# Cross attention and a gated feed-forward on one core: the transposed scores of batches 0 and 1 in one four-bank visit

## The chip, the cores and the metric

The kernel runs on one core of a Trainium2 chip. The metric is the device time of one execution in microseconds (us); the time of a kernel is the median of its runs. A profile is one further execution, recorded by the hardware profiler; its span goes from the first to the last instruction.

The engines are named as the profile names them: PE (matrix products; PEld its weight loads), DVE (vector), ACT (scalar functions), POOL (general), SP (here only an issuer of DMAs). Each works through its own instructions in order and waits on semaphores of the others.

## The reference

For each of B = 8 batches and H = 8 heads, `x` is 512 x 64 and `state` is 32 x 64:

```python
scale = 1.0 / np.sqrt(D)
a  = softmax(scale * x @ state.T)        # 512 x 32
xread = a @ state                        # 512 x 64
a2 = softmax(scale * state @ x.T)        # 32 x 512, the transposed scores
sread = a2 @ x                           # 32 x 64
h = concat([xread, sread])               # 544 rows per batch, heads side by side: 512 columns
out = (sigmoid(h @ w_gate) * (h @ w_val)) @ w_out    # d_ff = 1536
```

The output has 8 x 544 = 4352 rows of 512 floats.

## The kernel before

**Tiling.** The program is written out by hand: the order of the calls in the source is the order on each engine. One *step* belongs to each batch b = 2..7, and one more, b = 8, to the 256 rows of `sread` of all batches. A step is a loop over f = 0..11 (L696 to L744), one *group* for each 128 columns of d_ff. In a group PE makes `gv_mm(b, f)` (L275): gate and value for 128 columns by 512 rows, four 128x512 matmuls, and `out_mm(b - 1, f)` (L305), four matmuls of the output product of the batch before. In the last two steps `out_mm` comes first in each group. ACT makes the tanh of the gate (`gv_th`, L290), DVE multiplies it with the value (`gv_glu`, L295), and after every third group ACT moves an output bank to `res` (L318), from which SP writes 256 KB to DRAM (L320).

**The transposed scores** of a batch k ride in those groups. They go through these functions:

- `cT_mm(k)` (L175): eight matmuls with a 64x32 tile of PE's array each, four by two tiles, into two PSUM banks (e = 0, 1).
- `cT_max(k, e)` (L185): DVE takes the maximum of a bank (`cm`, L188) and makes the bias `nb` (L190).
- `cT_exp(k, e)` (L192): ACT writes the exponentials to `cE` and their sums to `cs` (L196).
- `cT_nrm(k, e)` (L198): DVE takes the reciprocal `rc` of the sums (L201), and POOL multiplies it in and writes `cN` (L204).
- `c_dma(k)` (L206): two DMA transposes on SP's queue, `cN` to `Eb` (L209).
- `sr_mm(k)` (L211): sixteen matmuls of 64 columns, `Eb` with `x`; `sr_cp` (L219) copies the two halves of the result to `XS`, one on ACT and one on DVE (L221). `XS` of all batches is what step 8 works on.

The tiles `cE`, `cs`, `nb`, `cN` and `Eb` come from a pool with two buffers of each name, so a third one waits until an earlier one has been read.

**Where they stand.** Batch b + 1 is done in the last five groups of step b (`col`, L385). Batches 0 and 1 are left for step 7: `col(0, t)` in groups 0 to 4, `col(1, t)` in groups 3 to 7, so that in groups 3 and 4 both are at work. Their order within a group is batch 0 first:

```python
for k in range(2):
    if 0 <= f - 3 * k < 5:
        col(k, f - 3 * k)
    elif f == 8 + 3 * k:
        sr_mm(k, SWP)
        sr_cp(k, 0, act)
        sr_cp(k, 1, vec)
```

`sr_mm(7)` stands in group 9 of step 7, its copies in group 10.

**PSUM.** Eight banks: two for gate and value (GV: one group's worth), one for the output (OU), four that rotate (SWP), one more (AT). In step 7 the scores of batches 0 and 1 and the `sr` results take SWP banks. `out_mm` starts a new output bank in groups 0, 3, 6 and 9, and has only the one bank OU, so it waits until ACT's `res` copy has emptied it.

Of the kernel before, what the change touches and what calls it, by code (L numbers as in the profile page):

```python
# [16 lines left out]
def kernel(  # L17
# [14 lines left out]
    nc = tc.nc  # L32
    B, H, S, D = x.shape
# [30 lines left out]
    AT, OU, GV, SWP = (p_at, "at"), (p_out, "outp"), (p_gv, "gv"), (p_sw, "swp")  # L64
    xfs, xbs, xTs = {}, {}, {}
    Es, E1s, Ebs, abs_, aTs, SWs, glus = {}, {}, {}, {}, {}, {}, {}
    vec, act, pool = nc.vector.tensor_copy, nc.scalar.copy, nc.gpsimd.tensor_copy
# [42 lines left out]
    def at_xT_dma(b):  # L110
        xT = xT_tile(b)
        for c in range(4):
            nc.sync.dma_start_transpose(xT[:, :, c], xbs[b][:, c].rearrange("p h d -> p (h d)"))

    def S_mm(b, i, place, jjs=(0, 1)):
        if jjs[0] == 0:
            held["S", b, i] = place[0].tile((128, 4, 2, 2, Ns), FP, name="Sp", tag=place[1])
        ps = held["S", b, i]
        for jj in jjs:
            for c in range(4):  # L120
                nc.tensor.matmul(ps[:, c, :, jj], xTs[b][:, 2 * i + jj, c], sTz[:, b, 2 * i + jj], start=True, stop=True)  # L121

    def S_max(b, i):

        if b not in E1s:
            E1s[b] = ap_.tile((128, 4, 2, 4, Ns), FP, name="E1")
        ps = held["S", b, i].rearrange("p c e j n -> p (c e) j n")
        mx = held["mx", b, i] = ap_.tile((128, 8, 2), FP, name="mx")
        nc.vector.tensor_reduce(mx, ps, AX.X, ALU.max)  # L129

    def S_sub(b, i):

        mx, ps = held["mx", b, i], held["S", b, i].rearrange("p c e j n -> p (c e) j n")
        nc.vector.tensor_tensor(halfE(b, i), ps, mx.unsqueeze(3).to_broadcast((128, 8, 2, Ns)), ALU.subtract)  # L134

    def S_exp(b, i):
        nc.scalar.activation(halfE(b, i), halfE(b, i), AF.Exp, scale=scale)  # L137
# [4 lines left out]
    def n_sum(b, i):  # L142
        rs = ap_.tile((128, 8, 2), FP, name="rs")
        nc.vector.tensor_reduce(rs, halfE(b, i), AX.X, ALU.add)  # L144
        ri = held["ri", b, i] = ap_.tile((128, 8, 2), FP, name="ri")
        nc.vector.reciprocal(ri, rs)  # L146

    def n_mul(b, i, eng, lo=0, n=4):
        if b not in abs_:
            abs_[b] = ap_.tile((128, 4, 2, 128), BF, name="ab")  # L150
        ri, ce = held["ri", b, i], slice(2 * lo, 2 * lo + 2 * n)
        eng.tensor_tensor(abs_[b].rearrange("p c e (j n) -> p (c e) j n", n=Ns)[:, ce, 2 * i:2 * i + 2],  # L152
                          halfE(b, i)[:, ce], ri[:, ce].unsqueeze(3).to_broadcast((128, 2 * n, 2, Ns)), ALU.mult)
# [17 lines left out]
    def aT_dma(b):  # L171
        for c in range(4):
            nc.sync.dma_start_transpose(aT_tile(b)[:, c], abs_[b][:, c].rearrange("p e k -> p (e k)"))

    def cT_mm(b, places):  # L175

        pss = [p[0].tile((128, 512), FP, name="cTp", tag=p[1]) for p in places]
        for j in range(4):
            for e in range(2):
                rows = slice(e * 64, (e + 1) * 64)  # L180
                nc.tensor.matmul(pss[e][j * Ns:(j + 1) * Ns], sTz[rows, b, j, e],  # L181
                                 xTs[b][rows, j].rearrange("p c t -> p (c t)"), start=True, stop=True)
        held["cT", b] = pss

    def cT_max(b, e):  # L185

        mx = ap_.tile((128, 1), FP, name="cm")
        nc.vector.tensor_reduce(mx, held["cT", b][e], AX.X, ALU.max)  # L188
        nb = held["nb", b, e] = ap_.tile((128, 1), FP, name="nb")
        nc.vector.tensor_scalar(nb, mx, -scale, None, op0=ALU.mult)  # L190

    def cT_exp(b, e):  # L192

        ex = held["cE", b, e] = ap_.tile((128, 512), FP, name="cE")
        cs = held["cs", b, e] = ap_.tile((128, 1), FP, name="cs")
        nc.scalar.activation(ex, held["cT", b][e], AF.Exp, bias=held["nb", b, e], scale=scale, accum_out=cs)  # L196

    def cT_nrm(b, e, eng):  # L198

        rc = ap_.tile((128, 1), FP, name="rc")  # L200
        nc.vector.reciprocal(rc, held["cs", b, e])  # L201
        if ("cN", b) not in held:
            held["cN", b] = ap_.tile((128, 2, 512), BF, name="cN")
        eng.tensor_scalar(held["cN", b][:, e], held["cE", b, e], rc, None, op0=ALU.mult)  # L204

    def c_dma(b):  # L206
        Ebs[b] = ap_.tile((128, 4, 2, 128), BF, name="Eb")
        for e in range(2):
            nc.sync.dma_start_transpose(Ebs[b][:, :, e], held["cN", b][:, e])  # L209

    def sr_mm(b, place):  # L211
        sr = held["sr", b] = place[0].tile((128, 4, 2, Ns), FP, name="srp", tag=place[1])
        Eb = Ebs[b].rearrange("p c e (j n) -> p c e j n", n=Ns)
        for j in range(4):
            for c in range(4):
                nc.tensor.matmul(sr[:, j], xbs[b][:, c, 2 * j:2 * j + 2].rearrange("p h d -> p (h d)"),  # L216
                                 Eb[:, c, :, j], start=(c == 0), stop=(c == 3))

    def sr_cp(b, e, cp):  # L219
        rows = slice(e * 64, (e + 1) * 64)  # L220
        cp(XS[rows, :, b * Ns:(b + 1) * Ns], held["sr", b][rows, :, e])  # L221
# [46 lines left out]
    def sw_cp(b, lo, w, e, cp):  # L268
        cp(*sw_left.pop((b, lo, w, e)))  # L269
# [115 lines left out]
    def col(b, t):  # L385

        if t == 0:
            cT_mm(b, (AT, SWP) if b > 1 else (SWP, SWP))
            cT_max(b, 0)
        elif t == 1:  # L390
            cT_max(b, 1)
            cT_exp(b, 0)
        elif t == 2:
            cT_exp(b, 1)
        elif t == 3:
            cT_nrm(b, 0, nc.gpsimd)
        else:
            cT_nrm(b, 1, nc.gpsimd)
            c_dma(b)

    def row(b, t):

        if t == 0:
            S_mm(b, 0, AT)
            S_max(b, 0)
        elif t == 1:
            S_sub(b, 0)
            S_mm(b, 1, SWP)
            S_max(b, 1)
        elif t == 2:  # L410
            S_sub(b, 1)
            S_exp(b, 0)
        elif t == 3:
            S_exp(b, 1)
            n_sum(b, 0)
            n_mul(b, 0, nc.gpsimd)
        elif t == 4:
            n_sum(b, 1)
            n_mul(b, 1, nc.gpsimd)
        else:  # L420
            aT_dma(b)
# [274 lines left out]
    for b in range(2, B + 1):  # L696
        nb = b + 1 if b + 1 < B else None
        for f in range(NF):

            v, q = divmod(f, 6)  # L700
            if nb is not None and q == 0:
                sw_wide(nb, v)
                sw_cp(nb, v, 0, 0, act)
                sw_cp(nb, v, 0, 1, act)
            ahead = nb is not None and q == 0
            for first in (ahead, not ahead):
                if first:
                    gv_mm(b, f, SWP if b == B and f % 2 else GV)
                    gv_th(b, f)
                    gv_glu(b, f)  # L710
                elif b < B or f < 9:
                    out_mm(b - 1, f)
            if nb is not None:
                if q == 0:
                    sw_cp(nb, v, 1, 0, vec)
                if q in (1, 3, 4):
                    k = max(q + 1, 3)
                    sw_cp(nb, v, k // 2, k % 2, act)
                if f == 10:
                    sr_cp(b, 0, act)  # L720
                    sr_cp(b, 1, vec)
                if 0 <= f - (b < 4) < 6:
                    row(nb, f - (b < 4))
                elif f >= 7:
                    col(nb, f - 7)
                if f == (6 if b > 3 else 3) and nb + 2 < B:
                    load_x(nb + 2, nc.sync, 4 if nb + 3 == B else 1)
                if f == (1 if b > 2 else 6) and nb + 1 < B:
                    cast_x(nb + 1, pool, 0, 4)
                    cast_x(nb + 1, pool, 4, 4)  # L730
                    at_xT_dma(nb + 1)
            if b < B and f == 9:
                sr_mm(b, SWP)
            if b == B - 1:
                if f == 10:
                    sr_cp(b, 0, act)
                    sr_cp(b, 1, vec)
                for k in range(2):
                    if 0 <= f - 3 * k < 5:
                        col(k, f - 3 * k)  # L740
                    elif f == 8 + 3 * k:
                        sr_mm(k, SWP)
                        sr_cp(k, 0, act)
                        sr_cp(k, 1, vec)  # L744
    for k in range(6):
        out_mm(B, k)
    out_last(B - 1, 3)
# [30 lines left out]
```

## Time and profile before

| | us |
|---|---|
| median of 3 runs | 232.07 |
| lowest and highest run | 231.16, 232.13 |
| the profiled execution's own time | 230.65 |
| its span, first to last instruction | 228.9 |

| engine | busy in the span, us |
|---|---|
| PE | 219.1 |
| ACT | 143.1 |
| DVE | 138.0 |
| POOL | 71.4 |

Step 7 fills about 176 to 199.5 us of the span, step 8 the time from there to 218 us. In a row of the timeline stand the start, the time that the group of instructions takes, the engine, the line, the operation and its tiles, the count, and in brackets how long the engine sat idle just before and what ended that. A matmul's time includes the way through the array: four 128x512 matmuls show 1.03 us, but the next ones start 0.86 us after them. A row that counts x3 where four were issued has lost a record. In a row of the chain stand the start, the time, and the engine with its tile and line.

### The profile page before, as it was taken

To read this page: it belongs to the slowest core of one execution; us is meant where nothing else is said; L and a number is where in the kernel's file an instruction comes from. 1 tells how busy PE (TensorE), PEld (TensorE's weight loads), DVE (VectorE), ACT (ScalarE), POOL (GpSimd) and SP (SyncE) were. 2 spreads that over 40 slices of the span, in tenths; PEclk is the share of its full clock that TensorE was granted. 3 is DMA by queue.
4 is the path that set the end of the run, shared out by engine and by line. 5 is a ranking of instruction groups with operands and counts; after the bars stand their busy time and mean duration, and the time that the engine had idled before them with its cause. 6 is when DMAs were issued, how large, how long until landed. Compare 5 with 4: busy or idle time off the path is not lost.

```text
span 228.9 us, 5007 instructions
## 1 busy us (share of the span) xinstructions
PE 219.1 (96%) x1885; PEld 111.5 (49%) x1911; DVE 138.0 (60%) x266; ACT 143.1 (63%) x288; POOL 71.4 (31%) x77
## 2 busy tenths in 40 slices
PE   8868999999999999999999999999999999999994
PEld 7653444434444444444444444445444434566744
DVE  0889779766587557666766577648755664422311
ACT  3588787677575866676767767584857655422411
POOL 3986371240507080307130533031301355000001
PEclk9999999999999999999999999999999999999999
DMA  6999979935794374842443766313121312411114
GB/s 215 269 201 285 206 88 182 269 85 126 209 292 134 61 181 94 246 148 74 92 126 83 238 84 142 89 46 87 57 46 75 99 37 69 116 39 77 46 26 115
DMA packets 47271, 29.49 MB, mean 129 GB/s; under 512 B 29872, under 2 KB 42544, under 8 KB 47248
## 3 DMA queue, kind: packets, MB, share of 16 engines
q1 hardware_dynamic: 40096, 21.84, 36.5%
q0 software_dynamic: 6864, 7.14, 17.0%
q8 instruction: 15, 0.25, 0.4%
q10 hardware_dynamic: 288, 0.20, 0.3%
q14 instruction: 8, 0.07, 0.1%
HBM read 18.35 MB, written 8.91 MB: 119 GB/s over the span
## 4 chain that ended last, share of the span: by engine, by line
PE 84%; DMA 7%; ACT 2%; issue 2%; POOL 2%; SPq 1%; DVE 0%; ACTq 0%
PE outp L314 36%; PE gvp L283 34%; PE swp L231 5%; PE gvp L286 5%; DMA wg<-in_moe_w_gate_dram 4%; DMA xf<-in_x_dram 2%; PE srp L216 2%; PE Sp L121 1%; SPq L74 1%; PE outp L334 1%; PE cTp L181 1%; POOL cN L204 1%; ACT res L318 1%; POOL xb L91 1%; ACT SW L269 1%
## 5 line engine op out<-in xcount | busy, mean ns | idle before, releaser
L298 DVE SCALAR_TENSOR_TENSOR glu<-th,gvp 128x512 bf16<-128x512 f32 (+1 forms) x108 | 70.3, 656 | 69.1 <-ACT th L293 52.8
L314 PE MATMUL outp<-wo,glu 128*128 128x512 bf16 x370 | 95.5, 379 | 1.7 <-issue 0.3
L283 PE MATMUL gvp<-aT,SW 128*128 128x512 bf16 x384 | 96.6, 379 | 0.3 <-DVE aT L169 0.3
L293 ACT ACTIVATE th<-gvp 128x512 f32<-128x512 f32 (+1 forms) x108 | 61.8, 576 | 51.2 <-PE gvp L283 41.4
L283 PEld LDWEIGHTS <-SW 128*128 128x128 bf16 x384 | 36.3, 98 | 44.8 <-issue 3.1
L314 PEld LDWEIGHTS <-glu 128*128 128x128 bf16 x396 | 36.5, 98 | 40.8 <-issue 3.2
L204 POOL TENSOR_SCALAR cN<-cE,rc 128x512 bf16<-128x512 f32 x16 | 24.9, 1564 | 66.2 <-DVE rc L201 53.4
L269 ACT CAST SW<-swp 128x512 bf16<-128x512 f32 x74 | 41.0, 586 | 3.5 <-PE swp L231 2.5
L152 POOL TENSOR_TENSOR ab<-E,ri 128x512 bf16<-128x512 f32 x16 | 16.7, 1047 | 48.4 <-DVE ri L146 21.7
L318 ACT ACTIVATE res<-outp 128x512 f32<-128x512 f32 x33 | 19.7, 597 | 16.8 <-PE outp L314 16.6
L269 DVE CAST SW<-swp 128x512 bf16<-128x512 f32 x22 | 14.7, 681 | 1.0 <-PE swp L231 1.0
L91 POOL CAST xb<-xf 128x1024 bf16<-128x1024 f32 (+1 forms) x14 | 13.6, 986 | 4.9 <-DMA xf<-in_x_dram 4.9
L196 ACT ACTIVATE cE<-cTp,nb 128x512 f32<-128x512 f32 x16 | 11.1, 694 | 0.8 <-POOL cN L204 0.8
L144 DVE TENSOR_REDUCE rs<-E 128x16 f32<-128x512 f32 x16 | 10.8, 675 | 0.7 <-ACT E L137 0.7
L188 DVE TENSOR_REDUCE cm<-cTp 128x1 f32<-128x512 f32 x16 | 10.9, 682 | 0.4 <-PE cTp L181 0.4
L137 ACT ACTIVATE E<-E 128x512 f32<-128x512 f32 x16 | 10.1, 637 | 1.6 <-DVE E L134 1.6
L129 DVE TENSOR_REDUCE mx<-Sp 128x16 f32<-128x512 f32 x16 | 10.7, 674 | 0.4 <-PE Sp L121 0.4
L134 DVE TENSOR_TENSOR E<-Sp,mx 128x512 f32<-128x512 f32 x16 | 10.9, 684 | 0.1
L325 POOL DMA_DIRECT2D out_dram<-res x2 | 1.1, 550 | 30.1 <-ACT res L318 30.1
L231 PE MATMUL swp<-wg,sTc 64*32 64x512 bf16 (+1 forms) x192 | 8.4, 328 | 0.2
L348 PE MATMUL warm<-ones 128*128 128x128 bf16 x87 | 7.6, 256 | 1.0 <-DVE ones L429 1.0
L231 PEld LDWEIGHTS <-sTc 64*32 64x32 bf16 x384 | 4.8, 91 | 7.4 <-issue 4.7
(62 smaller groups left out, 134.2 us busy)
## 6 DMA issues: line engine op xcount, KB each, us to landing
out_dram<-res SPq DMA_DIRECT2D x31, 256.0 KB, 2.4
xf<-in_x_dram SPq DMA_DIRECT2D x12, 256.0 KB, 4.8
xf<-in_x_dram SPq DMA_DIRECT2D x3, 1024.0 KB, 6.3
wo<-in_moe_w_out_dram POOLq DMA_DIRECT2D x3, 512.0 KB, 8.9
wv<-in_moe_w_val_dram POOLq DMA_DIRECT2D x2, 512.0 KB, 9.1
wg<-in_moe_w_gate_dram POOLq DMA_DIRECT2D x2, 512.0 KB, 10.1
xf<-in_x_dram POOLq DMA_DIRECT2D x2, 512.0 KB, 8.0
xf<-in_x_dram POOLq DMA_DIRECT2D x1, 1024.0 KB, 12.8
```

The costliest lines, as they stand in the source:

```text
L91: cp(xbs[b].rearrange("p c h d -> p h c d")[:, lo:lo + n], xfs[b][:, lo:lo + n])
L152: eng.tensor_tensor(abs_[b].rearrange("p c e (j n) -> p (c e) j n", n=Ns)[:, ce, 2 * i:2 * i + 2], halfE(b, i)[:, ce], ri[:, ce].unsqueeze ...
L196: nc.scalar.activation(ex, held["cT", b][e], AF.Exp, bias=held["nb", b, e], scale=scale, accum_out=cs)
L204: eng.tensor_scalar(held["cN", b][:, e], held["cE", b, e], rc, None, op0=ALU.mult)
L231: nc.tensor.matmul(pss[e][j * Ns:(j + 1) * Ns, o:o + n], sTc[rows, b, j] if b > 1 else sTz[rows, b, j, e], (wg, wv)[w][rows, j, lo:lo + n] ...
L269: cp(*sw_left.pop((b, lo, w, e)))
L283: nc.tensor.matmul(ps, SWs[b][:, g, w, fs], aTs[b][:, :, g], start=(g == 0), stop=(g == 1))
L286: nc.tensor.matmul(ps, (wg, wv)[w][:, j, fs], XS[:, j], start=(j == 0), stop=(j == 3))
L293: nc.scalar.activation(th, held["gv", b, f][0], AF.Tanh, scale=0.5)
L298: nc.vector.scalar_tensor_tensor(glus[b][:, f], held["th", b, f], 1.0, held["gv", b, f][1], ALU.add, ALU.mult)
L314: nc.tensor.matmul(ops[b, c], glus[b][:, f, c * 128:(c + 1) * 128], wo[:, f], start=(f == 0), stop=(f == NF - 1))
L318: nc.scalar.activation(res, ops[b, c], AF.Copy, scale=0.5)
```

## The change

Step 7 no longer uses `col` for batches 0 and 1, but a function of its own, `first01(f)`:

- In group 0 both batches' `cT_mm` are made one after the other, into all four SWP banks. Group 3 has no `cT_mm` any more.
- The maxima go to groups 0 to 3, one in each; the exponentials to groups 1, 3, 4 and 6 (before: 1, 2, 4, 5); the normalisations stay in groups 3, 4, 6 and 7. In group 3 the maximum of batch 1, e = 1 stands ahead of the reciprocal of batch 0, e = 0.
- `sr_mm(7)` and its copies go from groups 9 and 10 to group 5; `sr_mm(0)` goes from group 8 to group 9; `sr_mm(1)` stays in group 11. All three write the bank AT in place of an SWP bank.
- `c_dma(0)` goes from group 4 to group 6; `c_dma(1)` stays in group 7.

```diff
+    def sr_all(b, place):
+        sr_mm(b, place)
+        sr_cp(b, 0, act)
+        sr_cp(b, 1, vec)
+
+    def first01(f):
+
+        if f == 0:
+            for k in range(2):
+                cT_mm(k, (SWP, SWP))
+            cT_max(0, 0)
+        elif f == 1:
+            cT_max(0, 1)
+            cT_exp(0, 0)
+        elif f == 2:
+            cT_max(1, 0)
+        elif f == 3:
+            cT_max(1, 1)
+            cT_exp(0, 1)
+            cT_nrm(0, 0, nc.gpsimd)
+        elif f == 4:
+            cT_exp(1, 0)
+            cT_nrm(0, 1, nc.gpsimd)
+        elif f == 5:
+            sr_all(B - 1, AT)
+        elif f == 6:
+            c_dma(0)
+            cT_exp(1, 1)
+            cT_nrm(1, 0, nc.gpsimd)
+        elif f == 7:
+            cT_nrm(1, 1, nc.gpsimd)
+            c_dma(1)
+        elif f in (9, 11):
+            sr_all(f // 2 - 4, AT)
...
-            if b < B and f == 9:
+            if nb is not None and f == 9:
                 sr_mm(b, SWP)
             if b == B - 1:
-                if f == 10:
-                    sr_cp(b, 0, act)
-                    sr_cp(b, 1, vec)
-                for k in range(2):
-                    if 0 <= f - 3 * k < 5:
-                        col(k, f - 3 * k)
-                    elif f == 8 + 3 * k:
-                        sr_mm(k, SWP)
-                        sr_cp(k, 0, act)
-                        sr_cp(k, 1, vec)
+                first01(f)
```

## The prediction

> **What bounds the kernel now.** First the page: who is busy, and whose work makes up the chain that ended last.
>
> ```profile
> span 228.9 us, 5007 instructions
> PE 219.1 (96%) x1885; PEld 111.5 (49%) x1911; DVE 138.0 (60%) x266; ACT 143.1 (63%) x288; POOL 71.4 (31%) x77
> ...
> PE 84%; DMA 7%; ACT 2%; issue 2%; POOL 2%; SPq 1%; DVE 0%; ACTq 0%
> ```
>
> PE is the bound. Whatever the change does shows only as PE slots saved or added, and as PE idling. So the second view is the stage table, row of step 7 (start and end, length, then busy time of PE, PEld, DVE, ACT and POOL, the granted clock, the DMA share):
>
> ```profile
> 177.90:199.60 21.70, 21.26 (x152) 10.22 (x154) 11.50 (x26) 11.97 (x26) 7.72 (x5) 1.00 0.28 73
> ```
>
> DVE, ACT and POOL are half idle there; PE lacks 0.44 us of being always busy. Third, PE's timeline of that stage:
>
> ```profile
> 177.02 1.03 PE L283 MATMUL gvp<-aT,SW 128*128 128x512 bf16 x4
> 177.98 0.41 PE L181 MATMUL cTp<-xT,sTz 64*32 64x512 bf16 x8
> 178.32 1.04 PE L314 MATMUL outp<-wo,glu 128*128 128x512 bf16 x4
> 179.19 1.03 PE L283 MATMUL gvp<-aT,SW 128*128 128x512 bf16 x4
> ...
> 182.64 1.03 PE L283 MATMUL gvp<-aT,SW 128*128 128x512 bf16 x4
> 183.60 0.41 PE L181 MATMUL cTp<-xT,sTz 64*32 64x512 bf16 x8
> 184.17 0.81 PE L314 MATMUL outp<-wo,glu 128*128 128x512 bf16 x3 [0.16 <-issue]
> 184.82 1.03 PE L283 MATMUL gvp<-aT,SW 128*128 128x512 bf16 x4
> 185.68 1.03 PE L314 MATMUL outp<-wo,glu 128*128 128x512 bf16 x4
> 186.54 1.03 PE L283 MATMUL gvp<-aT,SW 128*128 128x512 bf16 x4
> 187.80 1.02 PE L314 MATMUL outp<-wo,glu 128*128 128x512 bf16 x4 [0.23 <-ACT res L318]
> ```
>
> Four 128x512 matmuls take a slot of 0.86 us (185.68 to 186.54). Two things stand out. A visit to the transposed scores costs 177.98 - 177.02 - 0.86 + 0.34 = 0.44 us of slots, and there are two. And group 6's output product, which could start at 186.54 + 0.86 = 187.40, starts at 187.80: a hole of 0.40 us. The chain of waits says what made the hole:
>
> ```profile
> 183.34 0.61 ACT th L293
> 183.94 0.94 issue
> 184.88 1.57 POOL cN L204
> ...
> 186.48 0.02 ACT cE L196
> 186.50 0.56 issue
> 187.07 0.19 ACT cE L196
> 187.26 0.50 ACT res L318
> ...
> 187.80 1.02 PE outp L314 x4
> ```
>
> Read it backwards. PE needs the output bank that ACT's `res` copy empties; ACT does that copy after the exponential of batch 1, e = 0; that exponential needs a `cE` buffer, and the older of the two is free only when POOL has normalised batch 0, e = 0; POOL waits for the reciprocal on DVE. The 0.94 us that the chain calls issue are DVE's:
>
> ```profile
> 183.97 0.69 DVE L298 SCALAR_TENSOR_TENSOR glu<-th,gvp 128x512 bf16<-128x512 f32 x1 [1.04 <-ACT th L293]
> 184.57 0.15 DVE L201 RECIPROCAL rc<-cs 128x1 f32<-128x1 f32 x1
> 184.64 0.67 DVE L188 TENSOR_REDUCE cm<-cTp 128x1 f32<-128x512 f32 x1
> 185.35 0.15 DVE L190 TENSOR_SCALAR nb<-cm 128x1 f32<-128x1 f32 x1
> ```
>
> So the hole hangs on **where the reciprocal stands in DVE's order of group 3**. Before, it comes directly behind `glu` of group 3, ahead of the maximum.
>
> **The change, part by part.**
>
> *One visit in place of two.* The kernel has such a double set already, early on: sixteen 64x512 matmuls in one go, two sets of weights on the same tiles, and a set of eight close by.
>
> ```profile
> 22.21 0.67 PE L231 MATMUL swp<-wg,sTz 64*32 64x512 bf16 x16 [0.56 <-DMA wg<-in_moe_w_gate_dram]
> 22.81 0.32 PE L369 MATMUL stp<-ident,sb 128*64 128x64 bf16 x8
> ...
> 24.54 0.41 PE L231 MATMUL swp<-wv,sTz 64*32 64x512 bf16 x8
> ```
>
> 0.67 against 0.41 us: the second set costs 0.26. Bounds: one matmul's streaming, 0.86 / 4 = 0.22 us, and a whole second visit, 0.44. I take 0.25. Group 1 thus starts 0.25 us later than before, and all that PE paces up to group 3 with it: `gv_mm` of group 3, its tanh, its `glu`. The second visit's 0.44 us in group 3 goes, but see below: it stands ahead of the hole.
>
> Against this stands a rule of the Trainium skill, TensorE: Matmul & The Clock Gate, section "Part 3: Packing small matmuls", "The mechanism": weight loads overlap running matmuls only where their row group differs. The second set uses the same two row groups as the first, so by that rule it would start like a new visit, 0.44 in place of 0.25, and the sum below would be 0.19 higher. The 0.67 us row speaks against it.
>
> *The order on DVE in group 3.* Now `cT_max(1, 1)` comes ahead of the reciprocal of batch 0, e = 0. So between `glu` of group 3 and that reciprocal stand a reduction and a bias. By the rows above the reduction occupies 184.64 to 185.35 = 0.71 us, and the bias, by the step from one short instruction to the next (184.57 to 184.64), 0.07; if the reciprocal has to wait for its whole length, 0.15. Together 0.78 to 0.86, taken as 0.82. The bias also waits for a free buffer, that is for the exponential of batch 0, e = 1, which ACT now makes in group 3, directly behind the tanh that `glu` waits for too; in the chain 0.78 us pass from one exponential to the copy behind it (186.48 to 187.26), less than `glu` and the reduction take together (183.97 to 185.35), so it is done first. No cost.
>
> Everything behind is a chain of fixed lengths, with no engine that could make it up: POOL 1.57, exponential, `res`, PE. So **PE resumes at 187.80 + 0.25 + 0.82 = 188.87 in place of 187.80, 1.07 us later.** `gv_mm`s of groups 4 and 5 aren't touched: they need only the tanh and `glu` of the group before.
>
> *`sr_mm(7)` goes from group 9 to group 5.* Its cost in a slot, before:
>
> ```profile
> 195.17 0.63 PE L216 MATMUL srp<-Eb,xb 128*128 128x64 bf16 x16
> 195.63 1.03 PE L314 MATMUL outp<-wo,glu 128*128 128x512 bf16 x4
> ```
>
> 0.46 us. Now it stands just ahead of group 6's output product, which is the hole: PE gets there at 187.40 + 0.25 - 0.44 = 187.21, is done with it at 187.67, and idles to 188.87. So the hole shows 1.2 us of idle time, and 0.46 us of work that had to be done anyway now lies in its shadow. It is the one real gain: **-0.46.** Its operand is there: `c_dma(7)` is the last thing of step 6.
>
> *The transposes on SP.* SP's queue holds, in order: the `res` write of group 5, both of batch 0, both of batch 1, the `res` write of group 8. The rows: the end of step 7 and the start of step 8 on PE; batch 1's products and transposes; the time to landing of all sixteen transposes.
>
> ```profile
> 199.55 1.03 PE L314 MATMUL outp<-wo,glu 128*128 128x512 bf16 x3
> 200.61 0.60 PE L286 MATMUL gvp<-XS,wg 128*128 128x256 bf16 x4
> ...
> 190.90 1.57 POOL L204 TENSOR_SCALAR cN<-cE,rc 128x512 bf16<-128x512 f32 x1 [2.27 <-DVE rc L201]
> 192.63 1.56 POOL L204 TENSOR_SCALAR cN<-cE,rc 128x512 bf16<-128x512 f32 x1 [0.17 <-DVE rc L201]
> ...
> 193.69 2.50 SPq L209 DMA_TRANSPOSE Eb<-cN  x2
> ...
> DMA to landing us min/median/max: 2.4/2.4/5.4
> ```
>
> Batch 0: POOL's second product ends at 184.88 + 1.07 + 2 x 1.57 = 189.09, the `res` copy that SP writes first at 187.76 + 1.07 = 188.83; with an estimated 0.6 for that write and 1.25 for the first transpose (half of 2.50) SP gets to the second at about 190.7, and it lands 2.4 later, 193.1. `sr_mm(0)` comes at 188.87 + 8 x 0.86 = 195.8: 2.7 us of slack. Batch 1: POOL's last product, 1.07 later than before, ends at 195.26, its transpose lands at 197.7. `sr_mm(1)`, at 199.55 - 0.46 = 199.09 before, comes 0.6 later: 2 us of slack. Before, the first of this pair (193.69) waited until `sr_mm(0)` had read its `Eb` buffer; now it takes batch 7's, free since group 5. That wait goes and is worth nothing, as POOL is later than it. The write of group 8's `res` is held up as before; `res` has four buffers. No cost.
>
> *The rest.* The exponential of batch 1, e = 1 moves to group 6, where POOL is done (189.09) before the tanh ahead of it is (about 190.9); its wait for POOL goes, but no hole of PE hung on it. The copies to `XS` change groups on engines that are half idle. Bank AT is empty each time: its copies are four groups or two ahead of the next use. The start of step 8 waits for the last `XS` copy as before (200.61 against 199.55 + 0.86 = 200.41: 0.2 us), since group 11 keeps its order.
>
> **The sum:** +0.25 + 0.82 - 0.46 = **+0.61 us**; by the bounds, +0.54 to +0.84. On the profiled execution's 230.65 that gives 231.26; on the median of the runs, 232.07, **232.7**. The profiled execution lies 0.51 under the lowest run, so runs scatter by as much as the change is worth. A difference under 0.5% (1.16 us) can't be told from no change here.
>
> **Rivals.**
>
> *The hole closes.* If POOL's product doesn't decide, the hole (0.40) goes and one visit is saved (0.44 - 0.25 = 0.19): -0.59, so 231.5. For it: fewer PE visits, and the exponentials are spread over more groups. Against it: the exponential of batch 1, e = 0 still stands in group 4, still third in two `cE` buffers, and what frees its buffer comes later on DVE. Chance 0.13.
>
> *The visit saves nothing* (the second set waits for its own weights, as in the rule above): +0.80, 232.9. Against it the x16 row. Chance 0.12.
>
> *Slower by more: the last transpose lands late.* Place: `sr_mm(1)` in group 11 of step 7, and behind it the first `gv_mm` of step 8. It decides from a landing of more than 2.4 + 2.0 = 4.4 us. At the longest in the trace, 5.4, PE waits 1.0 us: +1.6, 233.7. For it: the pair is issued later in time than before. Against it, the transposes in a window early on, where loads of `x` are in flight, and those of step 7, where none is:
>
> ```profile
> DMA to landing us min/median/max: 4.5/4.9/5.4
> ...
> DMA to landing us min/median/max: 2.4/2.4/2.4
> ```
>
> The long landings belong to the early window. Chance 0.09.
>
> *The forecast*, the POOL chain: 0.66.
>
> **How the numbers follow.** Predicted 232.7. The range reaches down to the first rival less half the distance of median and lowest run (231.5 - 0.45 = 231.05), and up to the last, 233.7. Faster by over 0.5% needs the first rival and scatter on top: 0.06. Slower by over 0.5%: the last rival, 0.09, and the upper end of the forecast and of the second with scatter, 0.07: 0.16. Within: 0.78.
>
> **What would show it.** In PE's timeline: x16 `cTp` in about 0.67 us at 178.0, then none; `srp` x16 at about 187.2; behind it `outp` with an idle of about 1 us put down to ACT `res`. On DVE in group 3: `glu`, `cm`, `nb`, `rc`. On ACT: the `cE` of group 4 behind an idle of more than 1 us put down to POOL. On SP: four `Eb` transposes in a row. From group 6 on PE runs 1.07 us late, from group 10 on 0.61. Wrong would be: no idle on ACT ahead of that `cE`, another long idle on PE after group 6, or a change in the 0.2 us at the start of step 8.

## The result, and the profile after

| | kernel before | changed kernel |
|---|---|---|
| median, us | 231.18 (22 runs) | 231.90 (22 runs) |
| lowest and highest run, us | 230.37, 232.25 | 230.89, 233.03 |
| ratio, with 95% interval | | 1.0035 [1.0021, 1.0049] |
| profiled execution: own time, span | 230.65, 228.9 | 232.31, 230.3 |

The change makes the kernel 0.35% slower, 0.81 us: by the interval 0.49 to 1.13 us, against +0.61 forecast. Over 22 runs the kernel before has a median of 231.18, 0.89 under that of the three runs shown ahead of the prediction.

The spans differ by 1.4 us, more than the ratio says. Where that is from shows at the first `cTp` visit of step 7: it starts at 178.77 us in the profile after, at 177.98 before, though everything up to there is the same program. So 0.79 us of the 1.4 were lost ahead of the change. From here on I count all stretches **from the start of that first visit**, which takes this out.

PE's timeline of the changed kernel, step 7:

```profile
177.81 1.03 PE L283 MATMUL gvp<-aT,SW 128*128 128x512 bf16 x4
178.77 0.62 PE L181 MATMUL cTp<-xT,sTz 64*32 64x512 bf16 x16
179.33 1.04 PE L314 MATMUL outp<-wo,glu 128*128 128x512 bf16 x4
...
187.11 1.03 PE L283 MATMUL gvp<-aT,SW 128*128 128x512 bf16 x4
187.97 0.63 PE L216 MATMUL srp<-Eb,xb 128*128 128x64 bf16 x16
189.66 1.02 PE L314 MATMUL outp<-wo,glu 128*128 128x512 bf16 x4 [1.06 <-ACT res L318]
...
200.49 0.63 PE L216 MATMUL srp<-Eb,xb 128*128 128x64 bf16 x16
200.95 1.03 PE L314 MATMUL outp<-wo,glu 128*128 128x512 bf16 x4
202.01 0.60 PE L286 MATMUL gvp<-XS,wg 128*128 128x256 bf16 x4
```

Three things are to be seen. There is one visit of sixteen, 0.62 us long; its slot is 179.33 - 177.81 - 0.86 = 0.66 us, against 0.44 for a visit of eight. The hole ahead of group 6 is there, ends on ACT's `res` copy as before, and is wider: 1.06 us of idle time in place of 0.23. And `srp` of batch 7 stands in it. Group 6 starts at 189.66 - 178.77 = 10.89 us after the visit (before: 187.80 - 177.98 = 9.82), so 1.07 later; step 8 at 202.01 - 178.77 = 23.24 (before: 200.61 - 177.98 = 22.63), so 0.61 later.

DVE's timeline of the same kernel, groups 3 and 4:

```profile
184.98 0.69 DVE L298 SCALAR_TENSOR_TENSOR glu<-th,gvp 128x512 bf16<-128x512 f32 x1 [0.25 <-ACT th L293]
185.58 0.68 DVE L188 TENSOR_REDUCE cm<-cTp 128x1 f32<-128x512 f32 x1
186.37 0.15 DVE L190 TENSOR_SCALAR nb<-cm 128x1 f32<-128x1 f32 x1
186.44 0.15 DVE L201 RECIPROCAL rc<-cs 128x1 f32<-128x1 f32 x1
186.70 0.69 DVE L298 SCALAR_TENSOR_TENSOR glu<-th,gvp 128x512 bf16<-128x512 f32 x1
```

The reciprocal starts 186.44 - 184.98 = 1.46 us after `glu` of group 3; before, 0.60. ACT's and POOL's timelines say what that does:

```profile
186.07 0.60 ACT L293 ACTIVATE th<-gvp 128x512 f32<-128x512 f32 x1 [0.46 <-PE gvp L283]
188.35 0.69 ACT L196 ACTIVATE cE<-cTp,nb 128x512 f32<-128x512 f32 x1 [1.68 <-POOL cN L204]
...
189.02 0.59 ACT L318 ACTIVATE res<-outp 128x512 f32<-128x512 f32 x1
```

```profile
186.75 3.10 POOL L204 TENSOR_SCALAR cN<-cE,rc 128x512 bf16<-128x512 f32 x2 [6.60 <-ACT th L293]
```

In the kernel before, ACT's two waits for POOL in step 7 were these:

```profile
186.48 0.69 ACT L196 ACTIVATE cE<-cTp,nb 128x512 f32<-128x512 f32 x1 [0.37 <-POOL cN L204]
188.66 0.69 ACT L196 ACTIVATE cE<-cTp,nb 128x512 f32<-128x512 f32 x1 [0.43 <-POOL cN L204]
```

Now ACT stands still for 1.68 us, in one place, until POOL's first product ends at 186.75 + 1.57 = 188.32; then come the exponential, the `res` copy and, 0.64 later, PE.

SP issues the four transposes in a row; these two answers give SP's timeline and the landing times in step 7 of the changed kernel:

```profile
190.07 7.21 SPq L209 DMA_TRANSPOSE Eb<-cN  x4
```

```profile
L209 SPq DMA_TRANSPOSE Eb<-cN x6: 1189/1193/1223, 178.6 to 196.1; - x6
...
DMA to landing us min/median/max: 2.4/2.4/2.4
```

The row that counts x6 has the two of batch 7 in it, ahead of the four. The 7.21 us are not all transfer: the third and the fourth start at 194.35 and 196.09, when POOL's products are done (192.76 + 1.56 and 194.50 + 1.56). The last one starts at 196.1 and lands 2.4 later, 198.5, against `sr_mm(1)` at 200.49: 2 us to spare.

### The profile page after: what moved, and what is told of

It is laid out like the page before. It is cut to its first block, busy times and chain, and to the rows that moved or that the text cites. A ratio compares the mean times of both kernels' runs of the same rounds, so it can differ in the third digit from the quotient of the medians.

```text
span 230.3 us, 5032 instructions
## 1 busy us (share of the span) xinstructions
PE 222.5 (97%) x1911; PEld 112.7 (49%) x1911; DVE 138.0 (60%) x266; ACT 142.9 (62%) x288; POOL 71.2 (31%) x77
## 4 chain that ended last, share of the span: by engine, by line
PE 88%; ACT 5%; DMA 2%; DVE 2%; issue 1%; POOL 1%; SPq 1%; ACTq 0%; DVEq 0%
PE outp L314 37%; PE gvp L283 34%; PE swp L231 5%; PE gvp L286 5%; DMA xf<-in_x_dram 2%; PE Sp L121 1%; PE srp L216 1%; ACT SW L269 1%; PE outp L334 1%; PE cTp L181 1%; PE xTp L105 1%; PE warm L348 1%; POOL cN L204 1%; ACT xT L108 1%; ACT res L318 1%
## 5 line engine op out<-in xcount | busy, mean ns | idle before, releaser
L314 PE MATMUL outp<-wo,glu 128*128 128x512 bf16 x396 | 99.0, 379 | 1.1 <-ACT res L318 1.1
L348 PE MATMUL warm<-ones 128*128 128x128 bf16 x87 | 8.2, 269 | 1.0 <-DVE ones L464 1.0
```

Of the source, the lines that this page charges most:

```text
L314: nc.tensor.matmul(ops[b, c], glus[b][:, f, c * 128:(c + 1) * 128], wo[:, f], start=(f == 0), stop=(f == NF - 1))
```

## The experiments

The theory: PE's hole ahead of group 6 hangs on a `cE` buffer that POOL frees, and POOL on where DVE takes the reciprocal; the wider hole is the loss, the `sr` matmuls in its shadow the gain, and the second set in the visit costs its streaming alone. Each run changes one of these. Since the steps are a few tenths of a microsecond, the traces decide, with stretches from the first `cTp` visit of step 7 to the start of group 6's output product and of step 8's first `gvp`; the ratios against the kernel before, each from runs of both taken together, stand beside them. Each trace is one execution only. But all eight differences to the kernel before that the traces give for step 8, from -0.81 to +1.48 us, lie inside the intervals of the ratios.

| kernel | group 6, expected | measured | step 8, expected | measured | ratio to before, 95% interval |
|---|---|---|---|---|---|
| before | | 9.82 | | 22.63 | 1 |
| changed | | 10.89 | | 23.24 | 1.0035 [1.0021, 1.0049] |
| reciprocal first | 10.03 | 10.04 | 22.38 | 22.38 | 1.0000 [0.9984, 1.0016] |
| four `cE` | 9.67 | 9.67 | 22.02 | 22.02 | 0.9980 [0.9965, 0.9996] |
| reciprocal later | 11.75 | 11.77 | 24.10 | 24.11 | 1.0093 [1.0053, 1.0133] |
| `sr_mm(7)` in group 7 | 10.89 | 10.90 | 23.70 | 23.71 | 1.0062 [1.0040, 1.0083] |
| two visits | 11.11 | 11.11 | 23.46 | 23.46 | 1.0041 [1.0023, 1.0059] |
| before, four `cE` | 9.42 | 9.44 | 22.23 | 22.25 | 0.9976 [0.9961, 0.9990] |
| four `cE`, copy on ACT | | | 21.83 | 21.82 | 0.9965 [0.9951, 0.9980] |

### The reciprocal first

```diff
         elif f == 3:
+            cT_nrm(0, 0, nc.gpsimd)
             cT_max(1, 1)
             cT_exp(0, 1)
-            cT_nrm(0, 0, nc.gpsimd)
```

> The changed kernel, with the normalisation of batch 0, e = 0 put ahead of the maximum of batch 1, e = 1 in group 3 of step 7. All stretches are counted from the start of the first cTp visit of step 7: group 6's output product starts at 9.82 us before and 10.89 after, step 8's first gvp at 22.63 before and 23.24 after. Theory (the hole of PE hangs on where the reciprocal stands in DVE's order): the reciprocal comes directly behind glu again, 0.86 us earlier, so group 6 starts at 10.03, step 8 at 22.38: 0.86 under the changed kernel, 0.25 under the kernel before. Rival (the hole comes from the visit of four banks, or from ACT's own order, not from DVE's): no move, 23.24.

DVE's timeline of this run, group 3, and ACT's wait:

```profile
184.45 0.69 DVE L298 SCALAR_TENSOR_TENSOR glu<-th,gvp 128x512 bf16<-128x512 f32 x1 [0.25 <-ACT th L293]
185.06 0.16 DVE L201 RECIPROCAL rc<-cs 128x1 f32<-128x1 f32 x1
185.13 0.67 DVE L188 TENSOR_REDUCE cm<-cTp 128x1 f32<-128x512 f32 x1
```

```profile
186.97 0.69 ACT L196 ACTIVATE cE<-cTp,nb 128x512 f32<-128x512 f32 x1 [0.82 <-POOL cN L204]
```

The reciprocal is back at 0.61 us behind `glu`, ACT waits 0.82 in place of 1.68, and step 8 starts at 200.63 - 178.25 = 22.38, 0.86 earlier than in the changed kernel. One line's place in the source is the whole loss, and more: with it first, the trace is 0.25 under the kernel before. In the ratio that difference can't be told from none.

### Four buffers for the exponentials

```diff
-        ex = held["cE", b, e] = ap_.tile((128, 512), FP, name="cE")
-        cs = held["cs", b, e] = ap_.tile((128, 1), FP, name="cs")
+        ex = held["cE", b, e] = ap_.tile((128, 512), FP, name="cE", bufs=4)
+        cs = held["cs", b, e] = ap_.tile((128, 1), FP, name="cs", bufs=4)
```

> The changed kernel, with four buffers in place of two for cE and cs; nothing else. Theory (the exponential of batch 1, e = 0 waits for a buffer that POOL must free): ACT doesn't wait there, PE has no hole ahead of group 6, which starts behind the sr matmuls at 9.67 us from the first cTp visit, and step 8 at 22.02: 1.22 under the changed kernel, 0.61 under the kernel before. Rival (ACT and DVE are too full in groups 3 to 5, buffers or not): a hole of 0.3 us or more stays, and step 8 doesn't come before 22.3.

PE's timeline, then ACT's, of this run:

```profile
186.16 1.03 PE L283 MATMUL gvp<-aT,SW 128*128 128x512 bf16 x4
187.02 0.63 PE L216 MATMUL srp<-Eb,xb 128*128 128x64 bf16 x16
187.49 1.03 PE L314 MATMUL outp<-wo,glu 128*128 128x512 bf16 x4
```

```profile
185.12 0.60 ACT L293 ACTIVATE th<-gvp 128x512 f32<-128x512 f32 x1 [0.46 <-PE gvp L283]
185.62 0.68 ACT L196 ACTIVATE cE<-cTp,nb 128x512 f32<-128x512 f32 x1
186.36 0.60 ACT L318 ACTIVATE res<-outp 128x512 f32<-128x512 f32 x1
```

The exponential follows the tanh at once, and the output product starts one `sr` slot (187.49 - 187.02 = 0.47) behind it: no hole. DVE's order is that of the changed kernel, so the late reciprocal alone costs nothing; it costs through the buffer. The edit gives `cs` four buffers as well, but `cE` is the one that counts: in the changed kernel ACT goes on at 188.35, 0.03 us after POOL's product, while the reciprocal, which reads `cs`, had begun at 186.44 and takes 0.15. The rival of full engines falls.

### The reciprocal later still

```diff
         elif f == 3:
             cT_max(1, 1)
             cT_exp(0, 1)
-            cT_nrm(0, 0, nc.gpsimd)
         elif f == 4:
+            cT_nrm(0, 0, nc.gpsimd)
             cT_exp(1, 0)
```

> The changed kernel, with the normalisation of batch 0, e = 0 moved one group later, to the head of group 4, so that its reciprocal stands behind glu of group 4 as well. The cost doubled: the reciprocal comes 0.86 us later (7.31 + 1.22 in place of 7.67 us from the first cTp visit), and all behind it. Theory: group 6 starts at 11.75, step 8 at 24.10, 0.86 over the changed kernel. Rival (something else than POOL ends the hole): step 8 stays at 23.24.

ACT's timeline of this run:

```profile
188.35 0.69 ACT L196 ACTIVATE cE<-cTp,nb 128x512 f32<-128x512 f32 x1 [2.55 <-POOL cN L204]
189.03 0.59 ACT L318 ACTIVATE res<-outp 128x512 f32<-128x512 f32 x1
```

The wait grows by 2.55 - 1.68 = 0.87, and step 8 by 0.87 (202.01 - 177.90 = 24.11). The delay passes to PE one for one. The ratio, 1.0093, is more than the 1.48 us of the trace (0.64%), but its interval, the widest of the table, holds that.

### `sr_mm(7)` outside the hole

```diff
-        elif f == 5:
-            sr_all(B - 1, AT)
...
         elif f == 7:
             cT_nrm(1, 1, nc.gpsimd)
+            sr_all(B - 1, AT)
             c_dma(1)
```

> The changed kernel, with the sr matmuls of batch 7 and their copies in group 7 in place of group 5, ahead of batch 1's transposes. Theory (in group 5 they lie in the shadow of the hole and cost nothing): group 6 starts at 10.89 us from the first cTp visit as in the changed kernel, behind a longer hole, and step 8 at 23.24 + 0.46 = 23.70. Rival (their place is worth nothing, since the sr matmuls cost their slot anywhere): 23.24.

PE's timeline of this run:

```profile
186.16 1.03 PE L283 MATMUL gvp<-aT,SW 128*128 128x512 bf16 x4
188.72 1.02 PE L314 MATMUL outp<-wo,glu 128*128 128x512 bf16 x4 [1.53 <-ACT res L318]
```

The hole ends at the same point (188.72 - 177.82 = 10.90) and is 0.47 longer; the matmuls' slot comes on top later, and step 8 starts at 201.53 - 177.82 = 23.71, 0.47 over the changed kernel. Their place in group 5 is worth their whole slot, as long as the hole is there.

### Two visits

```diff
         if f == 0:
-            for k in range(2):
-                cT_mm(k, (SWP, SWP))
+            cT_mm(0, (SWP, SWP))
             cT_max(0, 0)
         elif f == 1:
+            cT_mm(1, (SWP, SWP))
             cT_max(0, 1)
```

> The changed kernel, with batch 1's score matmuls in a visit of their own in group 1 in place of group 0. Stretches are counted from the start of the first cTp visit of step 7. Theory (a second set in the same visit costs only its streaming, 0.22 us, a visit of its own 0.44): group 3's glu, and with it the whole chain to PE, comes 0.22 us later; group 6 starts at 11.11, step 8 at 23.46. Rival (the second set waits for its own weights and costs as much as a new visit): no move, 10.89 and 23.24.

PE's timeline of this run:

```profile
177.96 0.41 PE L181 MATMUL cTp<-xT,sTz 64*32 64x512 bf16 x8
178.30 1.04 PE L314 MATMUL outp<-wo,glu 128*128 128x512 bf16 x4
179.17 1.03 PE L283 MATMUL gvp<-aT,SW 128*128 128x512 bf16 x4
180.13 0.41 PE L181 MATMUL cTp<-xT,sTz 64*32 64x512 bf16 x8
```

Step 8 starts at 201.42 - 177.96 = 23.46: the visit of its own costs 0.22 us more than the second set in a shared one. So the four-bank visit does save what its sharing promises, 0.22 us, and the second set costs 0.66 - 0.44 = 0.22, one matmul's streaming. The rule of the Trainium skill weighed in the prediction (TensorE: Matmul & The Clock Gate, "Part 3: Packing small matmuls", "The mechanism": weight loads overlap running matmuls only where the row group differs, or, as an earlier sentence there has it, where they go to a background weight buffer), read without its second half, would have made the two equal; these measurements decide against that reading. No run here shows whether such a buffer is what makes the second set cheap.

### The kernel before, with four buffers

The edit is that of the second experiment, made in the kernel before.

> The kernel before, with four buffers in place of two for cE and cs. Theory (the buffer that POOL must free made the hole there too): no hole ahead of group 6, which starts at 9.42 us from the first cTp visit in place of 9.82, and step 8 at 22.23 in place of 22.63: 0.40 us faster, 0.17%. Rival (the hole has another cause): 22.63.

PE's timeline of this run:

```profile
186.38 1.03 PE L283 MATMUL gvp<-aT,SW 128*128 128x512 bf16 x4
187.25 1.03 PE L314 MATMUL outp<-wo,glu 128*128 128x512 bf16 x4
```

The old hole goes as well (187.25 - 186.38 = 0.87, one slot), and step 8 comes 0.38 earlier. So with buffers enough on both sides the change is a gain: 22.25 to 22.02, 0.23 us, which is the saving of the visit. The intervals of the two ratios, 0.9976 and 0.9980, are too wide to show it.

### The version that beats both

```diff
-        sr_cp(b, 1, vec)
+        sr_cp(b, 1, act if b == 1 else vec)
```

on top of the four buffers in the changed kernel.

> The changed kernel with four buffers for cE and cs, and with both copies of the last sr result on ACT in place of one on ACT and one on DVE behind glu of group 11. Theory: no hole ahead of group 6 (step 8 would come at 22.02 us from the first cTp visit), and the 0.2 us that step 8 waits for DVE's copy goes too: 21.83, so 0.80 under the kernel before, 0.35%. Rival (ACT's second copy is as late as DVE's was): 22.0.

With four buffers alone, DVE makes the second copy behind `glu` of group 11:

```profile
198.77 0.69 DVE L298 SCALAR_TENSOR_TENSOR glu<-th,gvp 128x512 bf16<-128x512 f32 x1 [1.10 <-ACT th L293]
199.49 0.29 DVE L221 CAST XS<-srp 64x128 bf16<-64x128 f32 x1
```

Its copy ends at 199.78, and step 8 starts at 199.84. PE's and ACT's timelines of this run, with both copies on ACT, end of step 7:

```profile
199.07 1.03 PE L314 MATMUL outp<-wo,glu 128*128 128x512 bf16 x4
199.93 0.60 PE L286 MATMUL gvp<-XS,wg 128*128 128x256 bf16 x4
```

```profile
199.27 0.53 ACT L221 CAST XS<-srp 64x128 bf16<-64x128 f32 x2 [0.24 <-PE srp L216]
```

Step 8 follows the output product after one slot (0.86): ACT has both copies made at 199.80, which is 21.69 after the visit; DVE's was made 199.78 - 177.82 = 21.96 after it. Ratio 0.9965 [0.9951, 0.9980] to the kernel before, 0.46 to 1.13 us faster.

## Why the prediction was right

- **The sum.** Forecast +0.61, in the traces 23.24 - 22.63 = +0.61, by the ratio 0.49 to 1.13. The median 231.90 lies 0.8 under the 232.7 forecast because that number was built on the 232.07 of three runs; the 22 runs put the kernel before at 231.18, and 231.18 + 0.61 = 231.79. The median by itself could not have told the cases apart: the range of 231.05 to 233.7 had all the rivals in it, 231.90 is nearer to the 231.5 of "the hole closes" than to 232.7, and the interval of 0.49 to 1.13 also holds the +0.80 of "the visit saves nothing". The traces decide. That a difference under 0.5% can't be told from no change was too careful: with 22 runs of each kernel, 0.35% can.
- **The visit.** Taken +0.25; measured 0.22, the lower bound. Shown by the two-visits run.
- **DVE's order.** Taken 0.82 of 0.78 to 0.86; measured 1.46 - 0.60 = 0.86, the upper end, but not for the reason that was given for it. The reciprocal does start 0.07 behind the bias (186.37 to 186.44), as in the lower bound; it is the reduction's step to the bias that is 0.79 (185.58 to 186.37), not 0.71. The bias also waits for the exponential of batch 0, e = 1, which the prediction put down as no cost; ACT has that done well ahead (it starts at 184.84 and takes 0.68). The step is 0.78 to 0.79 at this bias in all seven profiles of the changed schedule, 0.70 to 0.72 at every other bias of step 7, before and after; what the 0.08 are wasn't tried. That the sum comes out to the hundredth is luck: the visit was taken 0.03 too dear, this step 0.04 too cheap, and the two cancel. 1.07 was forecast for group 6, and 1.07 measured.
- **The chain DVE, POOL, ACT, PE.** Shown from both sides: a reciprocal 0.86 earlier or 0.87 later moves step 8 by as much, and with buffers enough nothing is left of it.
- **`sr_mm(7)` in the hole.** Taken -0.46; 0.47 when it is moved out. Shown.
- **The transposes.** Slack of 2 us forecast for the last one, 2 us measured. The rival of a late landing did not come about: all landed in 2.4.
- **"The hole closes", -0.59.** It did not, but it was the right price for what four buffers do: -0.61.
- **The 0.2 us at the start of step 8** stayed: 202.01 - 200.95 - 0.86 = 0.20.

## What to carry to other kernels

Saving PE slots ahead of a hole saves nothing when the chain that ends the hole doesn't run through them: the second visit's 0.44 us went into the wait behind it. Even with the reciprocal first, group 6 started 0.22 us later than before (10.04 against 9.82), since the chain does run through group 0, where the second set went. When work of two items is interleaved on an in-order engine, look at what each tiny instruction releases: a 0.15 us reciprocal put behind a 0.7 us reduction delayed POOL, a buffer, ACT and PE one for one. And ask of a wait whether it is for data or for a buffer; two more buffers took 1.22 us off the changed kernel (23.24 to 22.02), the better place of the reciprocal 0.86.

## What the runs showed beside that

The start of the program scatters more than the change is worth: over these nine profiles the first `cTp` visit of step 7, with the same schedule up to there, starts between 177.81 and 178.77 us. The stage table of the first 20 us (start and end, length, busy times, then the granted clock, here 0.91 after, in the first row, and 1.00 before, in the second) differs as well:

```profile
0.00:20.00 20.00, 16.63 (x246) 13.15 (x247) 11.77 (x26) 12.10 (x23) 13.43 (x25) 0.91 1.10 221
```

```profile
0.00:20.00 20.00, 15.75 (x248) 12.10 (x249) 12.54 (x29) 12.96 (x24) 13.81 (x26) 1.00 1.11 227
```

The five profiles with 1.00 in this stretch reach the visit between 177.81 and 177.98, the four with 0.91 between 177.82 and 178.77. So the clock isn't the whole of it: with four buffers the changed kernel has 0.91 there too and reaches the visit at 177.82. What else sets the start was not tried. From the visit to step 8 the traces of the eight other kernels agree with what was expected of them to 0.02 us.
